# A block-wise FFT convolution with a SwiGLU FFN: block 1's filter rows loaded plainly and turned on TensorE, the loads of blocks 0 and 1 in one queue, the weights behind them

## The chip, the cores and the metric

The kernel runs on one NeuronCore of a Trainium2 chip. Five engines work side by side, each through its own list of instructions in a fixed order: TensorE (PE), VectorE (DVE), ScalarE (ACT), GpSimd (POOL) and SyncE (SP, which here only issues DMAs). An engine that has to wait for a semaphore holds everything behind it in its own list. The metric is the device time in microseconds (us) of one execution, lower is better.

## The reference, cut to what matters

```python
x = A_q                                   # [1, 2048, 640], bf16
q = layernorm(x)
k_shift = 4-tap causal filter of A_k along time (taps A_shift_k)
kv = k_shift * A_v
y = causal convolution over time of kv with A_ssm_k (one filter of 2048 taps per channel),
    written in the reference as rfft / product / irfft of length 4096
y = y + kv * A_ssm_D
h = x + q * y
g = silu(layernorm(h) @ w_gate); u = layernorm(h) @ w_up       # 640 -> 1728
out = h + (g * u) @ w_down                                     # 1728 -> 640
```

`A_ssm_k` lies in HBM as [640 channels, 2048 taps]: a row is a channel. The convolution needs it the other way round, taps on the partitions and channels along the row.

## The kernel before, in words

**Tiling.** The 2048 time steps are cut into four blocks `j` of 512, the 640 channels into two halves `c` of 320. Partition p of a block holds the steps 4p to 4p+3. Block 0 is convolved with dense transform matrices (`dense_c`, line 716; the matrices are the constant `cst_den`). Blocks 1 to 3 use a two-step transform (`conv_c`, line 1035): `kv_block` (line 909) makes kv on DVE, `fwd` (line 682) does the first step on PE for the filter (K) and for kv (X), with an eviction by ACT or DVE of each result, then four DMAs from SBUF to SBUF ("shuffles", line 699) regroup the partitions; `spec` (line 750) does the second step, `products` and `combine` multiply the spectra on DVE, `inv2` and the last matmuls in `conv_bp` go back. Block 1's `spec` may start only when the last dense matmul of block 0 is done (`d0_done`, line 756), because its result takes the place of the dense matrices. Then comes LayerNorm 1 (`ln_dve`, whose power -0.5 runs on POOL at line 866, and `ln_bp`, which transposes the result on PE at line 1061) and the FFN of the block (`ffn_f` with matmuls of 512 columns and Silu at line 1089, `ffn_b` with the down projection).

**Order.** The program first records operations with a priority (`P.op`), then `P.schedule` (line 131) simulates the engines and gives each operation a place in its engine's list: of those that are ready it takes the one of lowest priority number. FFN operations have 10000 and more for PE and so fill the gaps that the convolutions leave. Loads are placed with the arithmetic of `dma_model` (line 1173). The lists are then fixed; if a load is later on the chip than this arithmetic says, every engine with work on it placed next waits, and what is behind that work waits too.

**Tiles and slots.** `KRAW` is one slot for raw filter rows, `KT` three slots for turned filters, `KIN`, `VIN` one slot each for k and v, `XH` two for x. A slot's next user waits for the last reader of the one before. `TK`, two slots, first holds block 0's raw filter rows.

**Loads.** Block 0's (`load_front`, line 619) are issued by SP and ACT in the first 9 us: k, filter rows, v, the dense matrices, x, and last the tables `tab` of blocks 1 to 3. Block 0's filter rows are loaded as they lie and turned by 12 PE transposes per half (`k_first`, line 655, recorded at line 668), then evicted as two tiles of 128x640 (lines 544 and 545). For blocks 1 to 3, `load_kraw` (line 602) issues from SP one transposing DMA per half (line 605), then four shuffles `ksh` of 80 KB that put the four partition quarters of the result in their places; only when these have landed may the next transposing DMA use the slot. k and v of block 1 are issued by POOL after block 0's v has landed, x of block 1 by POOL after the first kv of block 0's second half. `load_weights` (line 1066) issues 14 pieces (6.6 MB) from POOL, each held until the last but one has landed, the first until block 0's first kv is done.

All plain DMAs are recorded at line 552, most matmuls at line 561, evictions at lines 544 (ACT) and 545/547, most DVE products and sums at line 760; LayerNorm 0's two passes over x are lines 889 and 896 on ACT.

Of the kernel before, what the change touches and what calls it, by code (L numbers as in the profile page):

```python
# [405 lines left out]
def bass_sequential_preLN__ssm_conv_h3__swiglu_ffn__prompt_kernel(  # L406
# [6 lines left out]
    R = 4  # L413
# [19 lines left out]
    with ExitStack() as es:  # L433
# [160 lines left out]
        def load_kv(j, prio):  # L594
            kt = kins[j] = P.tile(f"kin{j}", "KIN")
            vt = vins[j] = P.tile(f"vin{j}", "VIN")
            dma([(lambda: V(kt, 0, 7 * D), lambda: dram(K2, (B * j - 3) * D, [[R * D, 128], [1, 7 * D]]))], 1147, [], [(kt, c) for c in range(2)], prio,
                name=f"kin{j}", eng="pool", after=front["v0"] if j == 1 else ())
            dma([(lambda: V(vt, 0, 4 * D), lambda: dram(V2d, B * j * D, [[R * D, 128], [1, 4 * D]]))], 655, [], [(vt, c) for c in range(2)], prio + 1,
                name=f"vin{j}", eng="pool", after=front["v0"] if j == 1 else ())  # L600

        def load_kraw(j, c, prio):
            t = kraws[j, c] = P.tile(f"kraw{j}{c}", "KRAW")
            kt = kts[j, c] = P.tile(f"kt{j}{c}", "KT")
            P.op({"sp": 1.5}, [lambda g: g.dma_start_transpose(
                out=V2(t, 0, CW, 4, CW), in_=dram(A_ssm_k, c * CW * S + B * j, [[S, CW], [1, B]]))],
                [], [(t, 0)], prio, dma=(328, "turn"), name=f"kraw{j}{c}")
            for i in range(4):
                dma([(lambda i=i: V2(kt, 0, CW, 4, CW, 32 * i, 32 * i + 32), lambda i=i: V(t, i * CW, CW))], 82, [(t, 0)], [(kt, i)], prio,
                    name=f"ksh{j}{c}", kind="shuffle")  # L610

        def load_x(j, prio):
            t = xts[j] = P.tile(f"x{j}", "XH")
            dma([(lambda: V(t, 0, 4 * D), lambda: dram(X2, B * j * D, [[R * D, 128], [1, R * D]]))], 655, [],
                [(t, (b, c)) for b in range(4) for c in range(2)], prio, name=f"x{j}", eng="pool" if j else "sp", after=[kv_last[0, 1]] if j == 1 else ())

        front = {}

        def load_front():
            VIN0 = P.tile("v0", "TX")  # L620
            kins[0], vins[0] = KIN0, VIN0
            vec(0.7, lambda v: v.memset(V(KIN0, 0, 3 * D, 0, 1), 0.0), [], [(KIN0, "z")], -3000, name="kz")
            for c in range(2):
                kraws[0, c] = P.tile(f"kraw0{c}", "TK")

            def kin(p0, p1, o=0):
                return (lambda: V(KIN0, o * D, (7 - o) * D, p0, p1), lambda: dram(K2, (R * p0 - 3 + o) * D, [[R * D, p1 - p0], [1, (7 - o) * D]]))

            def kraw(c, prio):
                t, base = kraws[0, c], c * CW * S  # L630
                dma([(lambda: V2(t, 0, B, 2, B), lambda: dram(A_ssm_k, base, [[S, 128], [128 * S, 2], [1, B]])),
                     (lambda: V(t, 2 * B, B, 0, 64), lambda: dram(A_ssm_k, base + 256 * S, [[S, 64], [1, B]]))],
                    328, [], [(t, 0)], prio, name=f"kraw0{c}", eng="act")

            dma([kin(16, 128), kin(1, 16)], 1140, [], [(KIN0, "m")], -2001, name="kin0")
            dma([kin(0, 1, 3)], 10, [], [(KIN0, "s")], -2003, eng="act", name="kin0z")
            kraw(0, -2000)
            kraw(1, -1990)
            front["v0"] = [dma([(lambda: V(VIN0, 0, 4 * D), lambda: dram(V2d, 0, [[R * D, 128], [1, R * D]]))], 655, [], [(VIN0, c) for c in range(2)], -1990,
                               name="v0")]  # L640
            dma([(lambda: V(DROW, 0, D, 0, 1), lambda: dram(A_ssm_D, 0, [[D, 1], [1, D]]))], 1, [], [(DROW, 0)], -1980, name="drow")

            def den_piece(h, iv, prio):
                o = (iv * 4 + h) * 1024
                return dma([(lambda: sbh[:, DEN.base + o:DEN.base + o + 1024], lambda: den_dram.ap()[:, o:o + 1024])], 262, [], [(DEN, (iv, h))], prio, name=f"den{iv}{h}")

            for h in range(R):
                den_piece(h, 0, -1970 + h)
            load_x(0, -1960)
            for h in range(R):  # L650
                last = den_piece(h, 1, -1950 + h)
            front["den"] = [last]
            dma([(lambda: tab[:, :], lambda: tab_dram.ap())], 700, [], [(TAB, 0), (TAB, 1)], -1930, name="tab")

        def k_first(c, prio):
            kr = kraws[0, c]
            kt = kts[0, c] = P.tile(f"kt0{c}", "KT")
            pt = PT("pKT", "pC")
            fns = []
            for b in range(4):  # L660
                for d in range(3):
                    pr = 128 if d < 2 else 64

                    def f(t, b=b, d=d, pr=pr):
                        o = kr.base + d * B + b
                        a = sb[0:pr, o:o + 1]
                        src = bass.AP(a.tensor, a.offset, [list(a.ap[0]), [R, 128]])
                        return t.transpose(B16(pt, b // 2, (b % 2) * CW + d * 128, pr), src, V(IDN, 0, pr, 0, pr))  # L668

                    fns.append(f)  # L670
            pe(fns, 128, 37, [(kr, 0), (IDN, 0)], tc(pt), prio, reserve=[(kt, 0), (kt, 1)], name=f"ktr0{c}")
            for k in range(2):
                evac(lambda k=k: V(kt, k * 2 * CW, 2 * CW), lambda k=k: B16(pt, k, 0, 2 * CW), 2 * CW, [(pt[k], 0)], [(kt, 0)] if k == 0 else [(kt, 1)], prio, fast=True,
                     name=f"kte0{c}")
            d_add(c, kt, prio)

        def d_add(c, kt, prio):
            P.op({"pool": 1.0}, lambda g: g.tensor_tensor(out=V(kt, 0, CW, 0, 1), in0=V(kt, 0, CW, 0, 1),
# [37 lines left out]
        def dense_c(c):  # L716
            pb = 100 * c
            kv_block(0, c, pb + 100)
            k_first(c, pb + 102)
            xt = SXt[0, c] = P.tile(f"SX0{c}", "SX")  # L720
            kt = SKt[0, c] = P.tile(f"SK0{c}", "SK")
            kn = kts[0, c]
# [17 lines left out]

        def ksrc(j, c):
            kt = kts[j, c]
            return (lambda b: V(kt, b * CW, CW)), [(kt, i) for i in range(4 if j else 2)]

        d0_done = []

# [319 lines left out]
        def load_weights():  # L1066
            chain = []

            def piece(subs, kb, cells, nm):
                chain.append(dma(subs, kb, [], cells, 35, eng="pool", after=chain[-2:-1] or [kv_last[0, 0]], name=nm))  # L1070

            for q, (lo, hi) in enumerate(((0, 4), (4, 8), (8, 13))):
                for (nm, t, wd) in (("wg", WG, B_w_gate), ("wu", WU, B_w_up)):
# [6 lines left out]
            for a_, b_ in ((0, 3), (3, 6), (6, 9), (9, 11), (11, 13)):  # L1080
                piece([(lambda a_=a_, b_=b_: V2(WD, a_ * D, D, b_ - a_, D),
                        lambda a_=a_, b_=b_: dram(B_w_down, a_ * 128 * D, [[D, 128], [128 * D, b_ - a_], [1, D]]))], 164 * (b_ - a_),
                      [(WD, f) for f in range(a_, b_)], "wd")
            vec(0.4, lambda v: v.memset(V(WD, 13 * D, D, 64, 128), 0.0), [], [(WD, (13, "z"))], -3000, name="wz")
            vec(0.4, lambda v: v.memset(V(GUT, 13 * 512, 512, 64, 128), 0.0), [], [(GUT, (13, "z"))], -3000, name="gz")
            piece([(lambda: V(WD, 13 * D, D, 0, 64), lambda: dram(B_w_down, 13 * 128 * D, [[D, 64], [1, D]]))], 82, [(WD, 13)], "wdl")
# [55 lines left out]
            col(1)  # L1142
            dma([(lambda: dram(O2, (B * j + b) * D, [[R * D, 128], [1, D]]), lambda: V(xt, b * D, D))], 164, xc2, [], -900, name=f"st{j}{b}", kind="store")

        def block_j(j):
            pb = 1000 * j
            if j:
                load_kv(j, pb + 10)
                for c in range(2):
                    load_kraw(j, c, pb + 14 + 20 * c)  # L1150
                load_x(j, pb + 60)
            else:
                load_front()
            ln_act(0, j, pb + (300 if j else 95), range(4))
            for c in range(2):
                conv_c(j, c) if j else dense_c(c)
            for bp in range(2):
                ln_dve(1, j, pb + 400, range(2 * bp, 2 * bp + 2))
                ln_bp(j, bp, pb + 400)
            if j == 0:  # L1160
                load_weights()
# [5 lines left out]
        for j in range(NB):  # L1167
            block_j(j)


        link, turn = [2.6], [0.0]
# [1 line left out]
        def dma_model(o, issued, dmafree):  # L1173
            kb, kind = o.dma
            if kind == "shuffle":
                s = max(issued, dmafree[0])
                dmafree[0] = s + 0.3
                return s + 1.65 + (1.6 if link[0] > issued else 0.0)
            if kind == "store":
                return issued + 1.3  # L1180
            if kind == "turn":
                s = max(issued, link[0] + 1.0 if link[0] > issued + 2.0 else 0.0, turn[0])
                turn[0] = s + 4.9
                return turn[0]
            s = max(issued + (1.3 if o.eng == "pool" else 0.9), link[0])
            link[0] = s + kb / 345.0
            return link[0] + 1.0

        P.schedule(dma_model, 0.8)
# [35 lines left out]
```

## Time and profile before

| | |
|---|---|
| median of 3 runs (lowest, highest) | 331.1 us (329.04, 331.33) |
| the profiled execution: time; span, first to last instruction | 326.48 us; 324.8 us |
| mean granted TensorE clock in it | 0.967 |
| busy: PE, DVE, ACT, POOL | 288.9, 235.1, 194.4, 43.8 us |
| share of the chain that ended last: PE; DMA; ACT; SP's queue | 54%; 22%; 13%; 6% |
| transposing DMAs on SP | 6, 3.4 to 31.8 us from issue to landing |
| PE busy in the first 18 us, in 18 to 96 us, in 96 to 325 us | 7.1, 61.4, 220.5 us |

The times are those of the profiler's one execution. "Busy" is the time in which an engine executes; a wait is put down to what released it. The clock that the throttle granted to TensorE is given as a share of full speed. The last row is the sum of the windows' rows of PE: over the last 229 us PE is busy 96% of the time, before that it is not.

### The profile page before, as it was taken

The numbers are of one execution on the slowest core, as the hardware profiler recorded it, in microseconds if no ns is written. First come the engines' busy times: TensorE is split into PE (matmuls) and PEld (weight loads), VectorE is DVE, ScalarE is ACT, GpSimd is POOL, SyncE is SP. The second block draws the span as 40 slices with busy tenths as digits, with TensorE's granted clock in tenths as the row PEclk, the third lists the DMA queues.
The fourth block names the chain that finished last, engine by engine and source line by source line (L and its number), as shares of the span: only waits on it lengthen the run. The fifth ranks groups of instructions, "written<-read, shape, count | busy, mean of one in ns | idle before, by whom it ended". The sixth has DMA issues, their size and how long they took to land.

```text
span 324.8 us, 5118 instructions
## 1 busy us (share of the span) xinstructions
PE 288.9 (89%) x1820; PEld 154.1 (47%) x1820; DVE 235.1 (72%) x451; ACT 194.4 (60%) x470; POOL 43.8 (13%) x55
## 2 busy tenths in 40 slices
PE   3398859169899999989989999879999999999996
PEld 0165536043344445655434466544544477444574
DVE  1599848767869999898959999897369865233331
ACT  4169467289997783855973985389996414222200
POOL 0232223430112012300121001032010001000000
PEclk9999979758999999999999999998999999999999
DMA  7999889794667748742942211538120111000011
GB/s 192 356 405 145 118 242 253 214 327 165 163 173 153 193 104 182 202 143 81 281 84 42 83 41 49 175 112 195 40 79 4 40 63 42 20 0 0 2 40 40
DMA packets 32860, 42.58 MB, mean 131 GB/s; under 512 B 10642, under 2 KB 27699, under 8 KB 32325
## 3 DMA queue, kind: packets, MB, share of 16 engines
q1 hardware_dynamic: 25746, 23.63, 24.3%
q0 software_dynamic: 6240, 17.94, 22.8%
q10 hardware_dynamic: 850, 0.69, 0.8%
q8 instruction: 14, 0.23, 0.3%
q14 instruction: 10, 0.08, 0.1%
HBM read 19.97 MB, written 2.62 MB: 70 GB/s over the span
## 4 chain that ended last, share of the span: by engine, by line
PE 54%; DMA 22%; ACT 13%; SPq 6%; DVE 3%; issue 2%; ACTq 0%; DVEq 0%
PE ps L561 53%; DMA sb<-in_A_ssm_k_dram 12%; DMA sb<-sb 9%; ACT sb L544 7%; SPq L552 6%; DVE sb L760 2%; ACT sb L876 2%; ACT sb L547 2%; ACT sb L1089 1%; ACT sb L896 1%; PE ps L1061 1%; DVE stt L850 1%; DVE stt L854 0%; DVE sb L875 0%; DVE stt L868 0%
## 5 line engine op out<-in xcount | busy, mean ns | idle before, releaser
L561 PE MATMUL ps<-sb 128*128 128x320 bf16 (+2 forms) x1204 | 223.4, 339 | 10.1 <-ACT sb L544 7.0
L760 DVE TENSOR_TENSOR sb<-sb 128x1280 bf16<-128x1280 bf16 (+2 forms) x244 | 158.5, 701 | 24.4 <-ACT sb L544 8.8
L561 PEld LDWEIGHTS ps<-sb 128*128 128x128 bf16 (+2 forms) x1204 | 115.1, 99 | 101.1 <-ACT sb L544 9.1
L544 ACT ACTIVATE sb<-ps 128x320 bf16<-128x320 f32 (+1 forms) x262 | 100.8, 492 | 39.8 <-PE ps L561 26.7
L760 DVE TENSOR_TENSOR sb<-ps,sb 128x512 bf16<-128x512 f32 (+1 forms) x96 | 56.5, 603 | 50.9 <-PE ps L561 49.3
L561 PE MATMUL ps<-sb,tab 128*64 128x320 bf16 (+2 forms) x512 | 68.7, 320 | 12.1 <-DMA sb<-sb 9.2
L1089 ACT ACTIVATE sb<-ps 128x512 bf16<-128x512 f32 (+1 forms) x56 | 33.8, 604 | 45.9 <-PE ps L561 45.5
L561 PEld LDWEIGHTS ps<-sb,tab 128*64 128x64 f16 (+2 forms) x512 | 31.7, 104 | 51.0 <-issue 13.0
L876 ACT ACTIVATE sb<-sb,stt 128x320 bf16<-128x320 bf16 (+1 forms) x38 | 25.9, 742 | 12.6 <-DVE stt L868 12.6
L935 POOL DMA_DIRECT2D sb<-sb x12 | 12.3, 1021 | 71.8 <-DVE sb L760 63.5
L866 POOL TENSOR_TENSOR stt<-stt 128x2 f32<-128x2 f32 (+1 forms) x12 | 12.7, 1065 | 59.5 <-DVE stt L865 59.4
L547 ACT ACTIVATE sb<-ps 128x320 bf16<-128x320 f32 x48 | 17.5, 450 | 4.5 <-PE ps L561 4.5
L889 ACT ACTIVATE sb<-sb 128x640 bf16<-128x640 bf16 x16 | 11.9, 742 | 5.6 <-DMA sb<-in_A_q_dram 5.5
L850 DVE BATCH_NORM_STATS2 stt<-sb 128x6 f32<-128x320 bf16 x32 | 14.1, 476 | 0.0
L896 ACT ACTIVATE sb<-sb,stt 128x640 bf16<-128x640 bf16 x16 | 13.8, 863 | 0.1
L1061 PE MATMUL ps<-sb 128*128 128x128 bf16 x80 | 7.4, 248 | 4.1 <-ACT sb L544 4.0
L668 PE MATMUL ps<-sb 128*128 128x128 bf16 (+1 forms) x24 | 4.2, 283 | 6.6 <-DMA sb<-in_A_ssm_k_dram 6.6
L1061 PEld LDWEIGHTS ps<-sb 128*128 128x128 bf16 x80 | 5.8, 111 | 6.0 <-ACT sb L544 4.8
L668 PEld LDWEIGHTS ps<-sb 128*128 128x128 bf16 (+1 forms) x24 | 2.1, 118 | 9.2 <-DMA sb<-in_A_ssm_k_dram 7.3
L868 DVE TENSOR_TENSOR stt<-stt 128x2 f32<-128x2 f32 (+1 forms) x12 | 1.9, 156 | 5.7 <-POOL stt L866 5.7
L552 POOL DMA_DIRECT2D sb<-in_B_w_down_dram x6 | 4.3, 721 | 11.4 <-DMA sb<-in_B_w_down_dram 9.3
L552 POOL DMA_DIRECT2D sb<-in_A_q_dram x3 | 1.7, 576 | 29.7 <-ACT sb L547 20.7
(26 smaller groups left out, 40.6 us busy)
## 6 DMA issues: line engine op xcount, KB each, us to landing
sb<-sb SPq DMA_DIRECT2D x72, 160.0 KB, 2.3
sb<-sb POOLq DMA_DIRECT2D x12, 320.0 KB, 4.6
sb<-in_A_k_dram POOLq DMA_DIRECT2D x3, 1120.0 KB, 6.0
out_dram<-sb SPq DMA_DIRECT2D x16, 160.0 KB, 1.8
sb<-cst_den SPq DMA_DIRECT2D x8, 256.0 KB, 13.3
sb<-in_A_v_dram POOLq DMA_DIRECT2D x3, 640.0 KB, 6.0
sb<-in_A_q_dram POOLq DMA_DIRECT2D x3, 640.0 KB, 4.9
sb<-sb SPq DMA_DIRECT2D x24, 80.0 KB, 2.4
```

Of the source, the lines that this page charges most:

```text
L544: fns = {"act": lambda a: a.activation(out=dst(), in_=src(), func=ACTF.Copy), "dve": lambda v: v.tensor_copy(out=dst(), in_=src())}
L547: fns = {"act": lambda a: a.activation(out=dst(), in_=src(), func=ACTF.Copy, scale=scale), "dve": lambda v: v.tensor_scalar(out=dst(), in0 ...
L552: fns = [(lambda g, d=d, s=s: g.dma_start(d(), s())) for d, s in subs]
L561: return lambda t: t.matmul(o(), l(), r(), start=st, stop=sp)
L760: return lambda v: v.tensor_tensor(out=o(), in0=a(), in1=b_(), op=op)
L850: vec(dve1(CW, False), lambda v: v.bn_stats(st6(l, j, b, c), V(xt, b * D + c * CW, CW)), [(xt, (b, c))], [(ST, ("s", l, j, b, c))], prio, ...
L866: P.op({"pool": 1.05}, lambda g: g.tensor_tensor(out=y, in0=va, in1=stt[:, 420:420 + hi - lo], op=ALU.pow), c1 + [(ST, "half")], c3, prio, ...
L876: "act": lambda a: a.activation(out=dst(), in_=src(), func=ACTF.Identity, scale=rs(l, j, b), bias=tmv(l, j, 3)[:, b:b + 1])},
L896: P.op({"act": act_c(D) + 0.3}, lambda a, b=b, jt=jt: a.activation(out=V(jt, 0, D), in_=V(xt, b * D, D), func=ACTF.Square, bias=tmv(l, j, ...
L935: P.op({"pool": 1.0}, [lambda g: g.dma_start(v4(t0), src(), accum_op=ALU.add)], [(t0, 0)] + cells, [(t0, 0)], prio, dma=(656, "acc"), name ...
L1061: fns = [lambda t, k=k, d=d, pk=pk: t.transpose(B16(pk, 0, d * 128, 128), V(hn[k], d * 128, 128), V(IDN, 0, 128)) for d in range(5)]
L1089: P.op({"act": act_c(n)}, lambda a: a.activation(out=dst(), in_=src(), func=ACTF.Silu), rd, wr, -1000, name=f"si{nm}", after=after)
```

## The change

- Block 1's k, v and x are issued by SP (before: POOL), without the waits they had. By their priorities they stand in SP's list right behind block 0's loads and `tab`: k, v, filter rows of half 0, of half 1, x.
- Block 1's filter rows are loaded as they lie, by two plain DMAs per half (`kraw_rows`, which block 0 now uses as well), into the place of the first rows of w_down (`WD`). Two transposing DMAs and eight `ksh` shuffles go. The rows are turned by `k_turn` (the former `k_first`): 12 PE transposes and two evictions per half, recorded right after block 0's mixing.
- The weight chain on POOL starts when block 1's x has landed (before: at block 0's first kv); the pieces of w_down also wait for both turns.
- The recording is reordered (`loads_j`, `mix_j`, `ffn_j` in place of `block_j`), the priorities stay.
- The order's arithmetic takes 322 in place of 345 bytes per ns for the loads.

Blocks 2 and 3 keep their four transposing DMAs and their `KRAW` slot.

```diff
 def load_kv(j, prio):                       # kin and vin
-    ... eng="pool", after=front["v0"] if j == 1 else ())
+    ... eng="pool" if j > 1 else "sp")
+def kraw_rows(t, j, c, prio, eng):
+    base = c * CW * S + B * j
+    return dma([(lambda: V2(t, 0, B, 2, B), lambda: dram(A_ssm_k, base, [[S, 128], [128 * S, 2], [1, B]])),
+                (lambda: V(t, 2 * B, B, 0, 64), lambda: dram(A_ssm_k, base + 256 * S, [[S, 64], [1, B]]))],
+               328, [], [(t, 0)], prio, name=f"kraw{j}{c}", eng=eng)
 def load_kraw(j, c, prio):
+    if j == 1:
+        t = kraws[j, c] = P.tile(f"kraw{j}{c}", None, WD.base + c * 3 * B)
+        kraw_rows(t, j, c, prio, "sp")
+        return
 def load_x(j, prio):
-    ... eng="pool" if j else "sp", after=[kv_last[0, 1]] if j == 1 else ())
+    ... eng="pool" if j > 1 else "sp")
+    if j == 1:
+        front["x1"] = [o]
-def k_first(c, prio):
+def k_turn(j, c, prio):
-    pe(fns, 128, 37, [(kr, 0), (IDN, 0)], tc(pt), prio, reserve=[(kt, 0), (kt, 1)], name=f"ktr0{c}")
+    turned[j, c] = pe(fns, 128, 37, [(kr, 0), (IDN, 0)], tc(pt), prio, reserve=[(kt, 0), (kt, 1)], name=f"ktr{j}{c}")
-    d_add(c, kt, prio)
+    if j == 0:
+        d_add(c, kt, prio)
 def load_weights():
-    def piece(subs, kb, cells, nm):
-        chain.append(dma(subs, kb, [], cells, 35, eng="pool", after=chain[-2:-1] or [kv_last[0, 0]], name=nm))
+    def piece(subs, kb, cells, nm, after=()):
+        chain.append(dma(subs, kb, [], cells, 35, eng="pool", after=(chain[-2:-1] or front["x1"]) + list(after), name=nm))
     ...                                     # w_down's pieces:
-              [(WD, f) for f in range(a_, b_)], "wd")
+              [(WD, f) for f in range(a_, b_)], "wd", [turned[1, 0], turned[1, 1]])
+loads_j(0)
+mix_j(0)
+loads_j(1)
+for c in range(2):
+    k_turn(1, c, 1102 + 100 * c)
+load_weights()
+ffn_j(0)
+for j in range(1, NB):
+    if j > 1:
+        loads_j(j)
+    mix_j(j)
+    ffn_j(j)
 def dma_model(o, issued, dmafree):
-    link[0] = s + kb / 345.0
+    link[0] = s + kb / 322.0
```

More of the change, by code (lines that the diff above doesn't have):

```diff
@@ L597, in load_kv @@
             dma([(lambda: V(kt, 0, 7 * D), lambda: dram(K2, (B * j - 3) * D, [[R * D, 128], [1, 7 * D]]))], 1147, [], [(kt, c) for c in range(2)], prio,
-                name=f"kin{j}", eng="pool", after=front["v0"] if j == 1 else ())
+                name=f"kin{j}", eng="pool" if j > 1 else "sp")
             dma([(lambda: V(vt, 0, 4 * D), lambda: dram(V2d, B * j * D, [[R * D, 128], [1, 4 * D]]))], 655, [], [(vt, c) for c in range(2)], prio + 1,
-                name=f"vin{j}", eng="pool", after=front["v0"] if j == 1 else ())
+                name=f"vin{j}", eng="pool" if j > 1 else "sp")
+        def kraw_rows(t, j, c, prio, eng):
[3 more added lines that the diff above has]
+                       328, [], [(t, 0)], prio, name=f"kraw{j}{c}", eng=eng)
         def load_kraw(j, c, prio):
+            if j == 1:
+                t = kraws[j, c] = P.tile(f"kraw{j}{c}", None, WD.base + c * 3 * B)
+                kraw_rows(t, j, c, prio, "sp")
+                return
             t = kraws[j, c] = P.tile(f"kraw{j}{c}", "KRAW")
@@ L613, in load_x @@
             t = xts[j] = P.tile(f"x{j}", "XH")
-            dma([(lambda: V(t, 0, 4 * D), lambda: dram(X2, B * j * D, [[R * D, 128], [1, R * D]]))], 655, [],
-                [(t, (b, c)) for b in range(4) for c in range(2)], prio, name=f"x{j}", eng="pool" if j else "sp", after=[kv_last[0, 1]] if j == 1 else ())
-        front = {}
+            o = dma([(lambda: V(t, 0, 4 * D), lambda: dram(X2, B * j * D, [[R * D, 128], [1, R * D]]))], 655, [],
+                    [(t, (b, c)) for b in range(4) for c in range(2)], prio, name=f"x{j}", eng="pool" if j > 1 else "sp")
+            if j == 1:
+                front["x1"] = [o]
+        front, turned = {}, {}
         def load_front():
@@ L627, in kin @@
                 return (lambda: V(KIN0, o * D, (7 - o) * D, p0, p1), lambda: dram(K2, (R * p0 - 3 + o) * D, [[R * D, p1 - p0], [1, (7 - o) * D]]))
[L629 to L633, printed above, removed]
             dma([kin(16, 128), kin(1, 16)], 1140, [], [(KIN0, "m")], -2001, name="kin0")
             dma([kin(0, 1, 3)], 10, [], [(KIN0, "s")], -2003, eng="act", name="kin0z")
-            kraw(0, -2000)
-            kraw(1, -1990)
+            kraw_rows(kraws[0, 0], 0, 0, -2000, "act")
+            kraw_rows(kraws[0, 1], 0, 1, -1990, "act")
             front["v0"] = [dma([(lambda: V(VIN0, 0, 4 * D), lambda: dram(V2d, 0, [[R * D, 128], [1, R * D]]))], 655, [], [(VIN0, c) for c in range(2)], -1990,
@@ L653, in load_front @@
             dma([(lambda: tab[:, :], lambda: tab_dram.ap())], 700, [], [(TAB, 0), (TAB, 1)], -1930, name="tab")
-        def k_first(c, prio):
-            kr = kraws[0, c]
-            kt = kts[0, c] = P.tile(f"kt0{c}", "KT")
+        def k_turn(j, c, prio):
+            kr = kraws[j, c]
+            kt = kts[j, c] = P.tile(f"kt{j}{c}", "KT")
             pt = PT("pKT", "pC")
@@ L670, in k_first @@
                     fns.append(f)
-            pe(fns, 128, 37, [(kr, 0), (IDN, 0)], tc(pt), prio, reserve=[(kt, 0), (kt, 1)], name=f"ktr0{c}")
+            turned[j, c] = pe(fns, 128, 37, [(kr, 0), (IDN, 0)], tc(pt), prio, reserve=[(kt, 0), (kt, 1)], name=f"ktr{j}{c}")
             for k in range(2):
                 evac(lambda k=k: V(kt, k * 2 * CW, 2 * CW), lambda k=k: B16(pt, k, 0, 2 * CW), 2 * CW, [(pt[k], 0)], [(kt, 0)] if k == 0 else [(kt, 1)], prio, fast=True,
-                     name=f"kte0{c}")
-            d_add(c, kt, prio)
+                     name=f"kte{j}{c}")
+            if j == 0:
+                d_add(c, kt, prio)
         def d_add(c, kt, prio):
@@ L718, in dense_c @@
             kv_block(0, c, pb + 100)
-            k_first(c, pb + 102)
+            k_turn(0, c, pb + 102)
             xt = SXt[0, c] = P.tile(f"SX0{c}", "SX")
@@ L742, in ksrc @@
             kt = kts[j, c]
-            return (lambda b: V(kt, b * CW, CW)), [(kt, i) for i in range(4 if j else 2)]
+            return (lambda b: V(kt, b * CW, CW)), [(kt, i) for i in range(4 if j > 1 else 2)]
         d0_done = []
@@ L1143, in ffn_b, with loads_j @@
             dma([(lambda: dram(O2, (B * j + b) * D, [[R * D, 128], [1, D]]), lambda: V(xt, b * D, D))], 164, xc2, [], -900, name=f"st{j}{b}", kind="store")
-        def block_j(j):
+        def loads_j(j):
             pb = 1000 * j
@@ L1153, in block_j, with mix_j @@
                 load_front()
+        def mix_j(j):
+            pb = 1000 * j
             ln_act(0, j, pb + (300 if j else 95), range(4))
@@ L1159, in block_j, with ffn_j @@
                 ln_bp(j, bp, pb + 400)
-            if j == 0:
-                load_weights()
+        def ffn_j(j):
             for f in range(NFB):
@@ L1165, in block_j @@
                 ffn_b(j, b, 10000 + 100 * j)
-        for j in range(NB):
-            block_j(j)
+        loads_j(0)
[10 more added lines that the diff above has]
+            ffn_j(j)
         link, turn = [2.6], [0.0]
```

## The prediction

> **What bounds it now.** I read the page's table by slices first, then the chain that ended last in order of time, then the timeline around its long steps, then busy times by stage. Over the last 229 us PE is busy 96%, so what is to be had lies before 96 us. There the chain is not PE's (columns: start, length, what):
>
> ```profile
> 9.28 31.78 DMA sb<-in_A_ssm_k_dram
> ...
> 41.08 0.70 SPq L552
> ...
> 43.10 5.81 DMA sb<-sb
> ...
> 48.99 7.95 DMA sb<-in_A_ssm_k_dram
> 56.96 0.56 SPq L552
> ...
> 59.56 5.66 DMA sb<-sb
> ...
> 65.27 0.49 PE ps L561 x2
> ```
>
> From 9.28 to 56.96 us the chain is the two transposing DMAs of block 1's filter rows and, between them, the shuffles of the first that free their slot. Behind the second, SP's list holds four `ksh` issues (0.6 us each) ahead of shuffles that PE's `spec` at 65.27 needs. The timeline shows two stops (start, length; idle time before and its releaser in brackets):
>
> ```profile
> 42.95 0.74 ACT L889 ACTIVATE sb<-sb 128x640 bf16<-128x640 bf16 x1 [5.23 <-DMA sb<-in_A_q_dram]
> ...
> 44.16 5.04 PE L561 MATMUL ps<-sb 128*128 128x320 bf16 x24 [4.19 <-ACT sb L544]
> ...
> 65.27 2.61 PE L561 MATMUL ps<-sb,tab 128*64 128x320 bf16 x18 [7.18 <-DMA sb<-sb]
> ```
>
> First stop: block 1's x, issued at 27.93, lands only at 42.9; ACT stands 5.2 us before it with evictions queued behind, and PE stands 4.2 us for these. Second: PE stands 7.2 us for the shuffles. Stages (busy PE, PEld, DVE, ACT, POOL; clock; DMA share; GB/s):
>
> ```profile
> 26.00:34.00 8.00, 6.76 (x46) 4.00 (x46) 6.97 (x17) 6.25 (x17) 3.15 (x2) 1.00 1.12 145
> 34.00:42.00 8.00, 5.97 (x44) 4.08 (x42) 7.59 (x18) 3.48 (x8) 1.26 (x2) 1.00 0.67 124
> 42.00:49.00 7.00, 4.84 (x24) 2.92 (x24) 2.95 (x8) 5.48 (x14) 1.57 (x3) 0.76 0.88 249
> 49.00:58.00 9.00, 8.65 (x58) 5.23 (x56) 7.63 (x19) 7.19 (x22) 2.76 (x4) 1.00 0.87 221
> 58.00:65.00 7.00, 0.09 (x1) 0.00 (x0) 4.93 (x20) 0.91 (x3) 3.20 (x5) 0.72 0.89 249
> 65.00:82.00 17.00, 14.24 (x93) 6.85 (x93) 11.84 (x19) 16.19 (x37) 2.73 (x5) 0.71 0.77 247
> ```
>
> The DMA engines are occupied in 26 to 34 us but move 145 GB/s, against 372 in 9 to 18: that is the time of the first transposing DMA. After each stop the granted clock is low.
>
> **The change, term by term** (against the profiled execution, span 324.8, time 326.5 us).
>
> *First stop, -4.2 us.* x of block 1 no longer queues with a transposing DMA but stands in SP's ring ahead of all of them. Its landing: loads of block 0 and `tab` are 5.92 MB (sizes of the DMA issues), block 1's five are 3.11 MB, 9.03 MB together. The windows moved 1.83 MB to 9 us (203 GB/s), 3.35 to 18 (372) and 2.82 to 26 (353): 8.0 MB, so at 353 the rest lands near 29 us. If the ring alone only makes what SP and ACT's queues made from 3 to 11.5 us (293 on average of 323, 213, 281 and 342 GB/s; 2.7 MB moved), it is 11.5 + 6.3/0.293 = 33. The order's own arithmetic supposes 31.6, so ACT should wait 0 to 2 us. What is late next is the dense work itself, evicted at the pace seen before 40 us.
>
> *Second stop, -7.2 us.* Filter rows are in SBUF by 27 to 31 us. `spec` then waits for `d0_done`, the last dense matmul: 56.3 us now, less 4.2, plus the turns below. The X and K shuffles have from about 35 to 54 us to land. What covers the step is the dense work.
>
> *Clock, -1.0.* 42 to 49 us: 4.84 busy at 0.76 against 1.00 is 1.2 us lost. 65 to 82 us: 14.24 at 0.71 is 4.1 us lost, but ACT is busy 16.2 of 17 there, so I count nothing of it; bounds 0 and -4.1.
>
> *Turns, +3.0.* Block 0's show the price:
>
> ```profile
> 12.68 2.10 PE L668 MATMUL ps<-sb 128*128 128x128 bf16 x12 [5.76 <-DMA sb<-in_A_ssm_k_dram]
> ...
> 14.81 0.70 ACT L544 ACTIVATE sb<-ps 128x640 bf16<-128x640 bf16 x1 [6.37 <-PE ps L668]
> 14.81 0.49 DVE L545 COPY sb<-ps 128x640 bf16<-128x640 bf16 x1 [2.27 <-PE ps L668]
> ```
>
> Twelve are 2.1 us, so 4.2 for 24, at full clock. PE idles 1.24 us in 26 to 34 us, so 3.0 is on its path; bounds 0 (all in gaps) and 4.2. Four evictions of 0.49 or 0.70 are 2.0 to 2.8 us; ACT idles 4.5 us in 34 to 42 us, so nothing; without that cover, +2.8.
>
> *SP.* Eight `ksh` issues of 0.6 us go (4.8), seven plain issues of 0.35 to 1.1 come at 9 to 16 us, when SP has nothing else due: nothing beyond the second stop. But block 2's first transposing DMA has its slot free from the start and now stands behind x of block 1. The present one held SP from 9.28 to 25.13 and landed at 41.1, 12 us after `tab` in front of it. Placed behind x it lands near 29 + 12 = 41 to 45 us. Block 1's shuffles stand behind it in SP's list, and at 5.7 us each end by 51: hidden by the dense work until 54. Bounds 0 and, if it takes 31.8 us from the end of the ring (29 + 31.8 + 5.7 = 66.5 against 54), +12.5; I take 0, since later ones landed in 3.4 to 8.0.
>
> *POOL, +1.0.* The weights' first issue moves from 20.27 to about 29 to 33. From the second pair (39.6) to the last `gul` piece (54.7) it is 15.1 us now. Behind such pieces POOL's list holds LayerNorm 1's power for block 0:
>
> ```profile
> 63.00 0.76 POOL L552 DMA_DIRECT2D sb<-in_B_w_down_dram  x1 [3.78 <-DMA sb<-in_B_w_down_dram]
> 63.78 1.39 POOL L866 TENSOR_TENSOR stt<-stt 128x2 f32<-128x2 f32 x2
> ```
>
> It was ready at 60.6 and stood 3.2 us behind a piece. It will be ready near 55. The first pair took 19 us beside a transposing DMA; from 30 it lands between 36 (the 6.5 of an ordinary piece) and 49, so the piece ahead is issued between 51 and 64. I take the lower half: about the old wait, plus 1; bounds -3 and +9. w_down's wait for the turns (done by 45) binds nothing, and the FFN, which starts 77.5 now, meets its first weights by 49.
>
> *The rest, 0.* The additional places in the lists after 96 us are filled by FFN matmuls; the order there is made anew, which I bound by +-3.
>
> Sum: -4.2 - 7.2 - 1.0 + 3.0 + 1.0 = -8.4 us, 318.1 for the profiled execution. That one was 4.6 us under the median of 331.1; I take the saving from the median: **322.7 us**.
>
> A rule speaks against the second stop: the Trainium skill ("Advanced Engine Details and Errata", X-Bar Transpose) holds transposing DMAs to be as fast as plain ones, at 350 to 400 GB/s. The rows above say otherwise: 328 KB took 7.95 us, and 16 after SP was through with the issue. By the rule (an estimate: 0.9 us for a half) both loads would be short by themselves, and the sum would hold only the first stop, -1.2.
>
> **Rivals.**
>
> *POOL keeps the gain (0.16).* Power for block 0 runs at 64 again, because first weights start 9 to 13 us later and still meet a transposing DMA. The FFN's fill starts at 77 as now and PE has only block 1's evictions-bound work from 55 to 77. For: POOL's list is in order. Against: the trace's first pair was behind 9 us of other loads too. The second stop's 7.2 comes back: 322.7 + 7.2 = 330, within 1%.
>
> *The ring is slow (0.14, the slower side).* Everything for block 1 now hangs on one ring, and weights hang on its last member. At 213 GB/s, the lowest of the windows with SP and ACT alone, x lands at 11.5 + 6.3/0.213 = 41 us: DVE, PE (turns) and ACT each stand where the order supposed 24 to 32, 9 us. The first stop is then 9 instead of 4.2 (+4.8 beside the -4.2 not won), weights come 21 us later, and POOL's +9 applies for +1: 322.7 + 9 + 8 = 340. It decides from a landing after about 36 us. Against: 342 to 409 GB/s from 9 to 20 us, with POOL's share in it.
>
> *Nothing moves (0.04).* Were shuffles held by the weights' traffic and not by `ksh` and the transposing DMA, the stop would stay: 331. Their 5.7 us is such traffic, but the 47 us before are not.
>
> *More than the sum (0.20).* Clock loss goes wholly (-4.1), turns fit in gaps (-3.0): 322.7 - 7.1 = 315.6.
>
> **Numbers.** The forecast itself has 0.46. A measurement of this kernel can tell about 1% from no change. Faster by over 1% (under 327.8) are the forecast and the larger gain, with 0.05 of POOL's case: 0.71; within 1%: 0.14; slower: 0.15, with the new order's chance loss. The range leaves out the far end of the slow ring and the last of the larger gain: 312 to 334.
>
> **What would show it.** x of block 1 landed by 33 us and no wait of ACT at line 889 over 2 us; 48 transposes at line 668, the new ones 2.1 us a half; PE idle under 2 us between 40 and 66; `spec` before 57; FFN's first matmul near 69; clock 1.00 from 42 to 65. The prediction is wrong if PE waits at line 668 or `spec` for a transposing DMA of block 2, or if POOL's power at line 866 stands behind weights beyond 60 us.

## The result, and the profile after

| | before | after |
|---|---|---|
| median of all runs (lowest, highest) | 326.6 us of 27 (320.2, 332.5) | 326.2 us of 24 (324.4, 332.0) |
| the profiled execution: time; span | 326.48; 324.8 us | 326.85; 325.0 us |
| busy: PE, DVE, ACT, POOL | 288.9, 235.1, 194.4, 43.8 us | 290.5, 234.0, 199.6, 41.8 us |
| mean granted clock | 0.967 | 0.974 |

The forecast was 322.7 us. The measured ratio is 1.0095, with an interval of 1.0064 to 1.0127: 1% slower. (That ratio compares the runs within 1.5% of each kernel's fastest, and before's lie far apart, so everywhere below the medians of all runs stand beside it; by these the two kernels are level. The three runs of before that I started from were in the upper part of its spread.)

Nothing gained, then, but the profile is a different one. By stage, after (columns: stretch, its length; busy and number of PE, PEld, DVE, ACT, POOL; clock; DMA share; GB/s):

```profile
18.00:26.00 8.00, 8.00 (x48) 5.18 (x46) 4.58 (x9) 6.43 (x17) 1.06 (x1) 1.00 1.03 401
...
40.00:66.00 26.00, 22.14 (x148) 12.32 (x147) 21.18 (x55) 23.74 (x58) 9.68 (x12) 0.87 0.76 249
...
113.00:125.00 12.00, 12.00 (x85) 7.43 (x83) 12.00 (x32) 7.16 (x18) 2.22 (x2) 1.00 0.43 130
125.00:145.00 20.00, 19.56 (x156) 11.66 (x154) 19.97 (x31) 13.92 (x37) 1.05 (x2) 1.00 0.36 107
...
200.00:220.00 20.00, 12.11 (x91) 6.13 (x89) 17.36 (x39) 15.65 (x38) 4.93 (x5) 0.74 0.59 156
```

and the last four of these stretches before:

```profile
40.00:66.00 26.00, 14.30 (x86) 8.61 (x88) 17.64 (x48) 13.79 (x38) 9.28 (x12) 0.84 0.87 238
...
113.00:125.00 12.00, 11.85 (x70) 5.54 (x70) 11.93 (x21) 7.89 (x22) 2.11 (x2) 1.00 0.47 128
125.00:145.00 20.00, 18.74 (x153) 11.69 (x149) 18.00 (x40) 12.72 (x30) 3.47 (x4) 1.00 0.73 190
...
200.00:220.00 20.00, 17.05 (x142) 9.78 (x137) 17.73 (x40) 13.52 (x32) 4.52 (x5) 0.95 0.46 140
```

Read them in pairs. From 40 to 66 us PE now works 22.1 us, where before it worked 14.3: both stops are gone. From 113 to 145 us DVE has not a moment left (31.97 of 32 us). From 200 to 220 us PE works 12.1 us in place of 17.05, at a clock of 0.74: it stands 7.9 us there, in several waits, in place of 2.95. Busy time times clock is 9.0 against 16.2 us, so this stretch alone loses 7.2. It is told by PE's timeline of after (start, length; idle time before and its releaser in brackets):

```profile
207.30 1.19 PE L561 MATMUL ps<-sb,tab 128*64 128x320 bf16 x12 [1.08 <-DMA sb<-sb]
211.53 0.71 PE L1068 MATMUL ps<-sb 128*128 128x128 bf16 x5 [3.04 <-ACT sb L883]
213.74 0.72 PE L1068 MATMUL ps<-sb 128*128 128x128 bf16 x5 [1.50 <-ACT sb L544]
```

against the same place before:

```profile
211.39 2.75 PE L561 MATMUL ps<-sb 128*128 128x320 bf16 x19
214.07 0.46 PE L561 MATMUL ps<-sb,tab 128*64 128x320 bf16 x4
214.69 0.45 PE L1061 MATMUL ps<-sb 128*128 128x128 bf16 x5 [0.16 <-ACT sb L876]
```

The transposes of block 2's LayerNorm (line 1061 before, 1068 after) come at about the same time in both, 3 us sooner after. Before, the down projection of block 1 (the 19 matmuls of 320 columns) fills the time ahead of them; after, that FFN was over by 201 us and PE has nothing to put there. The chain that ended last shows what PE waits for; after, in order of time:

```profile
169.48 6.12 DMA sb<-sb
175.64 9.36 PE ps L561 x67
185.02 7.58 DVE sb L767 x12
193.19 3.50 DVE sb L767 x6
197.27 9.17 DVE sb L767 x16
...
211.38 1.72 ACT sb L883 x2
```

The transfer at 169.48 is the shuffles of the X of block 2's second half; behind PE's second step on it stand block 2's spectra on DVE (line 767, before 760), which end in block 2's rows. They are late because their input is: kv of block 2's second half has a higher priority number than the work of block 1 that is ready at that time, and in the full stretch above DVE had little time for it. Its four products with the taps start at 115.7, 128.2, 142.3 and 143.1 us (before 113.7, 114.8, 120.7, 122.1). Three accumulating DMAs from POOL add them up, the last of which lands at 161.9 (before 137.2), and the fifth and last product, with v, starts at 162.0 us in place of 150.2. PE's first step over it ends at 167.9 in place of 155.9.

The milestones of all that follows were read off the trace by taking each engine's list in order (us; the columns after the first two are experiments told below). The two rows on the ends of FFN 0 and 1 go by the start of their last weight load, since a few matmul records are missing in some of the traces.

| | before | after | order held | kv early | rate alone | kv late | 3 priorities |
|---|---|---|---|---|---|---|---|
| x of block 1 landed | 42.9 | 30.0 | 29.4 | 30.0 | 32.8 | 33.1 | 30.3 |
| `spec` of block 1 begins | 65.3 | 55.5 | 54.9 | 54.9 | 54.9 | 55.2 | 55.7 |
| first FFN matmul | 77.5 | 63.0 | 68.2 | 62.9 | 67.3 | 67.5 | 66.7 |
| last of FFN 0 | 150.4 | 141.5 | 139.5 | 141.1 | 139.9 | 140.2 | 139.6 |
| last product of block 2's kv, second half, starts | 150.2 | 162.0 | 140.1 | 131.2 | 142.8 | 150.1 | 125.2 |
| last of FFN 1 | 213.7 | 200.8 | 205.6 | 203.5 | 201.9 | 199.9 | 201.2 |
| rows of block 2 (h) done | 210.8 | 207.6 | 202.7 | 199.7 | 198.9 | 201.2 | 199.8 |
| first matmul of FFN 2 | 221.9 | 220.9 | 213.7 | 212.1 | 211.7 | 212.1 | 208.6 |
| median time | 326.6 | 326.2 | 318.1 | 317.5 | 319.1 | 326.4 | 315.4 |

After is 8.9 us ahead at the end of FFN 0 and 12.9 at the end of FFN 1, 3.2 in block 2's rows, and 1.0 where FFN 2 begins. That is where the gain goes. Why it goes there was tested.

### The profile page after: what moved, and what is told of

Same layout as the page of the kernel before. It is cut to its first block, busy times and chain, and to the rows that moved or that the text cites. A ratio compares the mean times of both kernels' runs of the same rounds, so it can differ in the third digit from the quotient of the medians.

```text
span 325.0 us, 5168 instructions
## 1 busy us (share of the span) xinstructions
PE 290.5 (89%) x1844; PEld 157.8 (49%) x1844; DVE 234.0 (72%) x447; ACT 199.6 (61%) x478; POOL 41.8 (13%) x52
## 4 chain that ended last, share of the span: by engine, by line
PE 54%; DMA 14%; DVE 13%; ACT 13%; SPq 2%; issue 2%; ACTq 1%; DVEq 0%
PE ps L561 53%; DVE sb L767 11%; DMA sb<-sb 10%; ACT sb L544 6%; DMA sb<-in_A_ssm_k_dram 4%; ACT sb L883 2%; SPq L552 2%; ACT sb L547 2%; ACT sb L1096 1%; PE ps L674 1%; ACT sb L903 1%; DVE stt L857 1%; ACTq L552 1%; PE ps L1068 1%; DVE sb L1027 0%
## 5 line engine op out<-in xcount | busy, mean ns | idle before, releaser
L544 ACT ACTIVATE sb<-ps 128x320 bf16<-128x320 f32 (+1 forms) x268 | 104.7, 486 | 37.5 <-PE ps L561 26.4
L561 PE MATMUL ps<-sb,tab 128*128 128x320 bf16 (+2 forms) x512 | 66.6, 313 | 13.1 <-DMA sb<-sb 9.8
L561 PEld LDWEIGHTS ps<-sb,tab 128*128 128x128 f16 (+2 forms) x512 | 32.2, 103 | 50.0 <-issue 14.2
L883 ACT ACTIVATE sb<-sb,stt 128x320 bf16<-128x320 bf16 (+1 forms) x40 | 27.6, 729 | 12.4 <-DVE stt L875 12.4
L873 POOL TENSOR_TENSOR stt<-stt 128x2 f32<-128x2 f32 (+1 forms) x12 | 12.1, 1015 | 95.5 <-DVE stt L872 95.5
L674 PE MATMUL ps<-sb 128*128 128x128 bf16 (+1 forms) x48 | 7.3, 254 | 6.7 <-DMA sb<-in_A_ssm_k_dram 6.6
L896 ACT ACTIVATE sb<-sb 128x640 bf16<-128x640 bf16 x16 | 12.1, 753 | 1.7 <-DMA sb<-in_A_q_dram 1.6
L674 PEld LDWEIGHTS ps<-sb 128*128 128x128 bf16 (+1 forms) x48 | 4.2, 117 | 10.6 <-DMA sb<-in_A_ssm_k_dram 7.4
L872 DVE TENSOR_SCALAR stt<-stt 128x2 f32<-128x2 f32 (+1 forms) x12 | 1.9, 162 | 6.4 <-ACT sb L903 6.4
L882 DVE TENSOR_SCALAR sb<-sb,stt 128x640 bf16<-128x640 bf16 (+1 forms) x8 | 3.8, 476 | 0.9 <-PE ps L1068 0.8
## 6 DMA issues: line engine op xcount, KB each, us to landing
sb<-in_A_v_dram SPq DMA_DIRECT2D x2, 640.0 KB, 12.6
```

Of the source, the lines that this page charges most:

```text
L544: fns = {"act": lambda a: a.activation(out=dst(), in_=src(), func=ACTF.Copy), "dve": lambda v: v.tensor_copy(out=dst(), in_=src())}
L561: return lambda t: t.matmul(o(), l(), r(), start=st, stop=sp)
L883: "act": lambda a: a.activation(out=dst(), in_=src(), func=ACTF.Identity, scale=rs(l, j, b), bias=tmv(l, j, 3)[:, b:b + 1])},
```

## The experiments

The theory: the change does what the prediction's terms say, and the order that the scheduler makes anew from another start gives it back. Its rival: the engines' totals set the end, so a stop removed early only comes back as another one later, in whatever order. Between the two stand the parts of the change: the plain rows, the one queue, the gate, the other rate.

"Order held" means that the scheduler takes an operation which exists in before only on the same engine and as that engine's next in before's sequence:

```diff
+    if o in held_order and held_order[o] != (e, nxt_held[e]):
+        continue
```

Free to find a place are only block 1's loads, the weight pieces and the new turns. All four kernels with the order held keep the rate of 322, which so places only these free operations.

### The whole change, the order held

After with the two lines above.

> The changed kernel, but every operation that the kernel before also has stands on the same engine and in the same order as there; only the loads that the change moves (block 1's k, v, x and filter rows, the weights) and the new turns are placed freely. Theory A (the front's gain is real; the order that was made anew gives it back between 145 and 220 us, where block 2's second kv comes 12 us later than before and PE then has nothing to fill with): block 0's and 1's steps early as in the changed kernel (spec of block 1 before 60 us, first FFN matmul before 70), block 2's second kv before 148 us, PE idle under 4 us between 200 and 218, time 3 to 6 us under the kernel before. Theory B (the later stages are bound by the engines' whole work, so a gain in front can't be carried): the same time as the changed kernel, 1% over the kernel before.

318.1 us (316.8 to 319.1), before beside it 326.7: -8.6 us, where 3 to 6 were expected. By stage, of this kernel:

```profile
200.00:220.00 20.00, 17.86 (x139) 9.32 (x139) 17.11 (x40) 17.25 (x41) 4.98 (x5) 0.91 0.60 165
```

Busy time times clock is 16.3 us there against after's 9.0, which is 7.3 of the 8.1 us that lie between the two, and block 2's rows are done at 202.7. The lead over before's profiled run stays between 8 and 11 us from `spec` (54.9) through FFN 0 (139.5) and block 2's rows to the end. By the medians the change is worth what was forecast, and the order costs 8.1 us on top of it: the theory holds, the rival falls. Of the two numbers the 8.1 is the firmer, as the runs of the two kernels lie apart (316.8 to 319.1 against 324.4 to 332.0 us); the 8.6 stands against the median of runs of before that lie between 319.2 and 328.8 us.

### One priority

After, in `kv_block`:

```diff
+    if (j, c) == (2, 1):
+        prio = 1100
```

(it was 2200; the smaller number goes first).

> The changed kernel with one priority altered: kv of block 2's second half (kv_block) has 1100 in place of 2200, so that DVE takes it ahead of block 1's and 2's other work. Theory A: its last product at about 135 us in place of 162, block 2's last convolved rows at about 201 in place of 207, FFN of block 1 ends near 204 in place of 201, PE idle between 200 and 218 falls from 7.9 to under 4 us, and the time falls by 4 to 7 us against the changed kernel, so 1 to 2% under the kernel before. Theory B: within 1.5 us of the changed kernel, with the idle time elsewhere.

317.5 us (316.7 to 320.5), 8.7 less than after, where 4 to 7 were expected. The last product starts at 131.2, block 2's rows are done at 199.7, and:

```profile
200.00:220.00 20.00, 16.84 (x127) 8.78 (x128) 16.92 (x35) 16.61 (x40) 4.99 (x5) 0.91 0.55 144
```

No load and no turn differs from after; what differs is when DVE makes the kv of one half block. DVE is as full from 113 to 145 us as in after (32.00 us of 32), so what counts is not its load but what it takes first. The number also moves what is placed behind it, so the reverse was run as well (below).

### The rate alone

Before, with nothing but the new rate:

```diff
-    link[0] = s + kb / 345.0
+    link[0] = s + kb / 322.0
```

> The kernel before with only the order's arithmetic changed, 322 for 345; no operation is added, removed or moved to another engine, only the order is made anew. Theory A (a new order costs some us by itself): 2 to 6 us slower than the kernel before, the two stops in front as before (PE idle 10 us or more between 40 and 66 us). Theory B: within 1% of the kernel before.

319.1 us (317.9 to 322.9), 7.7 less than before: an expectation missed, and the largest surprise of the study, as this kernel still has both transposing DMAs and no gate. POOL's and SP's timelines of it, and the row of the second stop's place:

```profile
16.61 0.94 POOL L552 DMA_DIRECT2D sb<-in_B_w_gate_dram  x1
17.54 0.89 POOL L552 DMA_DIRECT2D sb<-in_B_w_up_dram  x1
```

```profile
9.34 17.10 SPq L605 DMA_TRANSPOSE sb<-in_A_ssm_k_dram  x1
31.12 3.13 SPq L552 DMA_DIRECT2D sb<-sb  x4
```

```profile
40.00:66.00 26.00, 20.07 (x132) 11.51 (x130) 23.18 (x57) 21.92 (x57) 9.77 (x12) 0.75 0.95 268
```

The new order puts POOL's first two weight pieces at 16.6 and 17.5 in place of 20.3 and 21.2 us. They landed at 25.3 and 30.1. `tab`, which is ahead of the transposing DMA in SP's queue, landed at 29.9, and the transposing DMA 1.2 us behind it, at 31.1; the shuffles behind it went out at 31.12. In before `tab` landed at 29.0 and the transposing DMA 12.0 us behind it, at 41.1, with the weights in flight beside it until 39.3 and 41.4. So the stops don't come from the transposing DMA by itself but from its meeting with the weights' first pair.

### The ring alone

Before's order held; after's k, v and x on SP and the weights behind x; the transposing DMAs and their eight `ksh` stay, no turns.

```diff
-    name=f"kin{j}", eng="pool", after=front["v0"] if j == 1 else ())
+    name=f"kin{j}", eng="pool" if j > 1 else "sp")
-    load_x(j, pb + 60)
+    load_x(j, pb + (60 if j > 1 else 12))
-    after=chain[-2:-1] or [kv_last[0, 0]]
+    after=chain[-2:-1] or front["x1"]
```

(v and x as k.)

> The order of the kernel before held, and of the change only the ring: block 1's k, v and x on SP behind block 0's loads, x ahead of the filter rows, the weights behind x; the filter rows still come by two transposing DMAs with eight shuffles. If the transposing DMA was slow only because POOL's transfers ran beside it, it lands near 31 us in place of 41, the first stop goes and the second is mostly gone (spec before 60 us): 2 to 5 us under the kernel before. If it is slow by itself, it lands at 40 us or later and spec stays at 62 us or later: the time of the kernel before within 1%.

323.0 us (319.5 to 324.5), -3.7. The first transposing DMA lands at 28.7, `spec` starts at 55.0, and then PE waits for shuffles after all (PE's timeline, and the stage's row):

```profile
76.75 1.39 PE L582 MATMUL ps<-sb,tab 128*64 128x320 bf16 x5 [5.37 <-DMA sb<-sb]
```

```profile
66.00:82.00 16.00, 10.58 (x48) 4.43 (x49) 9.98 (x16) 10.66 (x27) 1.98 (x3) 0.79 0.77 242
```

The next transposing DMA, of block 2, was issued at 56.92 and took 10.3 us beside the weights, with those shuffles behind it. The queue clears the first meeting and leaves a later one.

### Before, a second time

> The kernel before, unchanged, for a second profile. If its two stops belong to the kernel, the first transposing DMA lands at 40 us or later again, x of block 1 at about 43, and PE idles 10 us or more between 40 and 66 us. If they are of some executions only, the transposing DMA lands near 31 us as in the run with the rate alone, spec begins before 58 us, and the execution is 4 us or more shorter than 326.5.

One run, 327.6 us. The stage of the stops, to be held against the 14.30 us of PE's row above:

```profile
40.00:66.00 26.00, 14.58 (x88) 8.48 (x86) 18.15 (x49) 14.22 (x39) 8.06 (x11) 0.86 0.86 234
```

The transposing DMA landed at 41.6 and x at 44.0 (41.1 and 42.9 the first time). So the stops are not of one execution. Both profiled ones are of 326 to 328 us, however; whether before's runs of 320 us have them too is not shown.

### The rows alone

Before's order held; plain rows and turns as in after; k, v, x and the weights' start as in before.

```diff
+    if j == 1:
+        t = kraws[j, c] = P.tile(f"kraw{j}{c}", None, WD.base + c * 3 * B)
+        kraw_rows(t, j, c, prio, "sp")
+        return
```

> The order of the kernel before held, and of the change only the filter rows: loaded plainly from SP and turned on PE; block 1's k, v and x and the weights come from POOL as before. If the stops come from the transposing DMA running beside POOL's loads, both go with the transposing DMA: x of block 1 lands before 35 us, PE idles under 5 us between 40 and 66, 318 to 320 us as with the whole change in the held order. If the weights beside block 1's loads are at fault, x lands at 38 us or later and the time stays above 322.

317.8 us (316.7 to 319.5), -8.3 against 326.1; ratio 0.9892 [0.9775, 1.0008]. The weights go out at 20.0 as in before and land at 27.9 in place of 39.3, x lands at 34.3, and

```profile
40.00:66.00 26.00, 21.39 (x156) 13.68 (x156) 24.56 (x62) 22.18 (x56) 7.82 (x10) 0.90 0.61 191
```

Without the transposing DMA the same weights cause neither stop. By the medians this part by itself is worth the whole; the interval of the ratio just takes in no change.

### The weights alone

Before's order held, all as in before, but the first weight pieces wait for the first transposing DMA.

```diff
-    after=chain[-2:-1] or [kv_last[0, 0]]
+    after=chain[-2:-1] or front["kraw10"]
```

> The order of the kernel before held, its loads and transposing DMAs as they were; only the first two weight pieces wait until the first transposing DMA has landed (before: block 0's first kv). If the first transposing DMA is slow because the weights run beside it, it lands near 31 us, x of block 1 before 35, spec starts before 58 us and the time is 318 to 321. If it is slow by itself, it lands at 38 us or later and the time stays within 1% of the kernel before.

Four runs at 317.3, 319.0, 324.1 and 325.9 us; ratio 0.9898 [0.9652, 1.0145], so no gain in time is shown. The transposing DMA lands at 26.9, x at 32.7, and `spec` starts at 55.2, so taking the weights away clears the two stops in front as taking the DMA away does. The profiled run (322.5 us of span) then loses 4.65 us of PE in 66 to 82, as the ring alone did; which runs do and which don't was not settled. The parts don't add up: -8.3 and -3.7 are -12.0, the two together -8.6, since both remove one meeting.

### The old rate with the change

After with `kb / 345.0`.

> The changed kernel with the order's arithmetic at the old 345 in place of 322; nothing else. Its order has block 2's second kv 5 us earlier than the changed kernel's. If the loss in the middle is a matter of the order, the time lies elsewhere than the changed kernel's 326.2, by my reading 2 to 5 us under it, with PE idle 4 to 7 us between 200 and 220. If the change itself costs it, within 1.5 us of 326.

334.1 us (333.7 to 338.6); ratio to before 1.0425 [1.0251, 1.06]. The expectation was missed in its sign: a time under after's was expected, and it is 8 us over. The front is nearly as good as after's (PE busy 22.3 us in 40 to 66, `spec` at 56.9), and the last product of block 2's kv starts at 171.4 us, the latest of all. But the loss is not where it was looked for: in the profiled run (338.6 us) PE stands only 1.9 us between 200 and 220. Its busy time times clock is 10.8 us short of after's already between 66 and 145 us, and FFN 0 ends at 154.0 against 141.5; what PE lacks there was not followed. The rate was a part of the change that I passed over; it changes nothing but the order, and between these two values it decides 8 us.

### The reverse of the one priority

The rate alone, with the same product later:

```diff
+    if (j, c) == (2, 1):
+        prio = 2260
```

> The kernel before with 322 in the order's arithmetic (319.05 us in its own run) and one more edit: kv of block 2's second half has priority 2260 in place of 2200, so that DVE takes it later. If that product's lateness by itself starves PE, its end moves from 143 to about 149 us, PE idles more between 195 and 225, and the time rises by 3 to 6 us to 322 to 325. If its place is without weight, 319 within 1.5 us.

326.4 us of 10 runs (324.6 to 333.0), 7.3 more than the rate alone, where 3 to 6 were expected; ratio to before 1.0107 [1.0049, 1.0164], nearly after's. The last product starts at 150.1 in place of 142.8, FFN 1 ends at 199.9, and the hole is after's:

```profile
200.00:220.00 20.00, 14.79 (x93) 7.30 (x93) 15.46 (x35) 16.11 (x38) 3.63 (x4) 0.74 0.37 109
```

Early in a slow order gives 8.7 us, late in a fast one takes 7.3: that this one number decides such sums is shown from both sides, with all that it moves behind it. The way is the same only in part. Busy time times clock is 10.9 in the stretch, where the rate alone has 15.7 (17.23 at 0.91); the rest of the loss goes with a second stop, of 4.25 us, ahead of block 3's transposes at 271.67, where the rate alone has one of 1.1 us and after none.

### Two better orders of the change

Three priorities of the kv products, in `kv_block` of after:

```diff
+    prio += {(1, 0): -1000, (2, 0): -95, (2, 1): -200}.get((j, c), 0)
```

> The changed kernel with three priorities of kv_block altered: block 1's first half by -1000, block 2's first by -95 and second by -200. If an early second kv of block 2 is what the changed kernel lacks: its end before 135 us, PE idle under 4 us between 200 and 220, 315 to 319 us. If the front's gain can't be carried: 324 or more.

315.4 us (313.5 to 317.0) against 326.3; ratio 0.9695 [0.9617, 0.9772]. The last product starts at 125.2 us, where "before 135" was said.

```profile
200.00:220.00 20.00, 17.06 (x127) 8.30 (x129) 16.00 (x34) 17.66 (x44) 5.00 (x5) 1.00 0.53 141
```

The other takes the rate and one priority of block 3:

```diff
+    prio += {(3, 1): -95}.get((j, c), 0)
-    link[0] = s + kb / 322.0
+    link[0] = s + kb / 360.0
```

> The changed kernel with the order's arithmetic at 360 in place of 322, and kv of block 3's second half 95 lower in priority number. Another order of the same work: with block 2's second kv ending near 143 us by this order I expect 315 to 320 us; a time over 324 would say that this product's place is not what decides.

316.5 us (315.6 to 318.3); 0.9719 [0.9651, 0.9788]; the last product starts at 142.1 us. Both beat both kernels. Orders of one and the same work (after, one priority, old rate, these two) span 315.4 to 334.1 us, with PE busy 285.3 to 290.5 us in four of them and 298.5 in the slowest, DVE 234.0 to 237.2.

## Why the prediction was wrong, point by point

**"The rest, 0 ... the order there is made anew, which I bound by +-3"** is the step that failed. It measured +8.1 us (326.2 after, 318.1 with the order held). I took the places in the lists after 96 us for filled, because PE was busy 96% there. They were, but with what was at hand: FFN 1 was used up by 201 us while DVE, full from 113 to 145, put off the one product on which block 2 hangs. A share near one says that the order of the time fits, not that a new one will. The old rate's 334.1 shows that even a bound of +-8 would have been short.

**The sum, -8.4**: right in its total, with luck. With the order held it is -8.6. But the terms as measured below (-4.2, -7.2, -2.9, at most +3.2, -3.2) add up to -14.3 (an estimate from these rows), so the errors of two terms, the clock's and POOL's, don't show in the total: the stops' lead of 10.4 us at `spec` is 8.1 us at block 2's rows, and what took the difference was not followed.

**First stop, -4.2**: right. x landed at 30.0 us, inside the 29 to 33 worked out, and ACT doesn't wait for it: its first pass over it, at what was line 889, starts at 42.9 in the new order.

**Second stop, -7.2**: right. `spec` starts at 55.5 in after and 54.9 with the order held, where "before 57" was said. Its reason was half right: the transposing DMA was slow through its company, as the runs with the rate alone, the rows alone and the weights alone show, and removing either side was enough to clear the stop.

**Clock, -1.0**: too small, by rows with the order held:

```profile
58.00:65.00 7.00, 4.50 (x34) 2.81 (x32) 5.16 (x9) 7.00 (x16) 3.76 (x5) 0.58 0.94 271
65.00:82.00 17.00, 15.96 (x96) 6.97 (x99) 14.05 (x22) 16.97 (x47) 3.38 (x5) 0.97 0.75 227
```

58 to 65 us at 0.58 with 4.50 us busy is 1.9 lost, 65 to 82 at 0.97 with 15.96 is 0.5. That is 2.4, before 1.2 + 4.1 = 5.3; so -2.9. "Clock 1.00 from 42 to 65" was wrong from 58 on: PE still stands 2.4 us there for evictions. PE's idle time in 40 to 66 is 3.9 us, not under 2.

**Turns, +3.0**: at most 3.2, as the price was put at 2.1 us a half and the trace has less:

```profile
42.34 1.58 PE L674 MATMUL ps<-sb 128*128 128x128 bf16 x12
...
53.36 1.58 PE L674 MATMUL ps<-sb 128*128 128x128 bf16 x12
```

**SP, 0**: right, from a wrong landing. Block 2's transposing DMA behind x was put at 41 to 45 us. It was quicker (SP's timeline of after):

```profile
17.42 9.01 SPq L615 DMA_TRANSPOSE sb<-in_A_ssm_k_dram  x1
```

It landed at 31.1, 13.7 us after its issue and 1.1 us behind the plain load of x in front of it. Here the rule that I had weighed, of the Trainium skill ("Advanced Engine Details and Errata", X-Bar Transpose: transposing DMAs as fast as plain ones), agrees with the trace: its estimate was 0.9 us a half. Beside the weights' first pair the trace still speaks against it: of the 31.8 and 32.2 us from issue to landing in the two profiles of before, 12.0 and 12.6 came after `tab` in front of it had landed, for the same 328 KB. So the 31.8 us were more than half a wait behind other loads, and what I had left out of the rest was the company.

**POOL, +1.0**: wrong in sign. The power for block 0 ran when DVE had made its input, not behind a piece:

```profile
55.21 2.21 POOL L873 TENSOR_TENSOR stt<-stt 128x2 f32<-128x2 f32 x2 [4.17 <-DVE stt L872]
```

The old 3.2 us behind a piece went; the first weights, issued at 34.0, landed in 5.1 us, as the transposing DMA was through.

**The rivals.** *POOL keeps the gain* would have shown the power at 64; it ran at 55.2. *The ring is slow* asked for x after 36; it landed at 30.0, and 401 GB/s stand in 18 to 26. *Nothing moves* had the right outcome and the wrong reason: the stop did go. *More than the sum* was half right: the clock gave 2.9 of its 4.1 us and the turns were cheaper by a quarter, yet with the order held the total was no larger than the forecast's. The slower side was right in sign only as a chance of the new order; no rival named it with a place and a price.

**The base.** The saving was taken from 331.1, the median of the three runs shown; 27 runs have 326.6. The same saving from there would be 318.2, close to the 318.1 that the order held gives, so this moved the number and not the outcome.

## What to carry to other kernels

Where a program orders the lists, a change of the front is two changes: the work that moves, and the order that is made anew from it. Price the second by itself: look for the engine that is full in the middle of the span, for the least urgent work on it, and for what hangs on that work, and hold the old order in an experiment before believing either sign. And a slow transfer is to be asked for its company before it is replaced: moving the neighbour may be enough.

## What the runs showed of the hardware

Unexpected was how little the DMA engines move in that meeting while they are occupied. DMA views, 25 to 41 us of before, by queue (packets, MB, share of 16 engines; q0 is POOL's, q1 holds the transposing DMA):

```profile
DMA packets 1463, 2.06 MB, mean 129 GB/s; under 512 B 1051, under 2 KB 1051, under 8 KB 1462
...
q0 software_dynamic: 448, 1.78, 58.9%
q1 hardware_dynamic: 1014, 0.27, 26.7%
```

and 34 to 41 us of the kernel in which the weights wait, where again a transposing DMA (6.7 us) and weights run together:

```profile
DMA packets 1698, 1.79 MB, mean 255 GB/s; under 512 B 1344, under 2 KB 1344, under 8 KB 1696
...
q0 software_dynamic: 384, 1.44, 69.1%
q1 hardware_dynamic: 1312, 0.33, 23.7%
```

One of POOL's packets of about 4 KB took 0.589 x 16 x 16 us / 448 = 0.34 us in the first and 0.691 x 16 x 7 / 384 = 0.20 in the second. So in before POOL's own packets (weights and x of block 1) were slowed too, and not by every transposing DMA beside them. Why in this one meeting, and whether it is what spreads before's runs over 12 us, stays open.
